# Block rows of the later query thirds: two heads copied by GpSimd, four by VectorE five slots later

## The chip, the cores and the metric

The kernel runs on one core of a Trainium2 chip. A core has five engines, each with an instruction stream of its own that it executes in order: TensorE (PE: matmuls and transposes, with weight loads, PEld, beside them), VectorE (DVE), ScalarE (ACT), GpSimd (POOL) and SyncE (SP, which here only issues DMAs). They wait for each other by semaphores. The metric is the device time of one execution in microseconds (us): 216.38 us, the median of three runs (216.07 to 217.03).

## What is computed

A block-sparse attention followed by a gated MLP with a spatial gate.

```python
# q, k, v: (4, 8, 768, 64) = batch, heads, sequence, head dim
scores = q @ k.T / sqrt(64)
mask   = |blk_i - blk_j| <= 1, or blk_i or blk_j the first or last of 24 blocks of 32,
         or blk_j one of 3 sampled blocks of blk_i      # the same for all batches and heads
attn   = softmax(where(mask, scores, -1e9)) @ v
x      = attn.transpose(0, 2, 1, 3).reshape(4, 768, 512)

h      = relu(x @ w_in)                  # 512 -> 1024
u, v   = h[..., :512], h[..., 512:]
v_n    = (v - mean(v)) / sqrt(var(v) + 1e-6)
v_s    = w_spatial @ v_n + b_spatial     # over the 768 positions
out    = (u * v_s) @ w_out               # float32 (4, 768, 512)
```

## The kernel before

**The mask as 24 more rows.** The scores of a head are matmuls over 88 rows of one tile, `kq` (88 x 8 heads x 1536, bf16): columns 0 to 767 are keys, 768 to 1535 queries. Rows 0 to 63 hold the head's transposed keys and queries. Rows 64 to 87 (`MR`, one for each of the 24 blocks) hold the block rows: for a key the block that it lies in, for a query a large negative number for each block that it may not see. So the product over 88 rows is the masked score, and the exponential follows directly. The block rows are the same for all heads and batches; they are built for head 0 and then copied to the other seven, once, by `rows(hs, cs, eng)` (L239 to L244: heads `hs`, columns `cs`). The rows of `kq` are reused for every later batch, so these copies happen only at the start.

**Thirds.** The 768 queries are cut in three thirds of 256 columns; `qcols(t0, n)` are the query columns of `n` thirds from `t0`. The heads go in pairs: pair 0 is heads 0 and 1, pair 3 heads 6 and 7. For the first batch (four pairs) the scores are made in twelve units of three slots (`UNITS`, L386): units 0 and 1 are the heads 0 and 1 with all thirds; units 2, 3, 4 the first third of pairs 1, 2, 3; units 5, 6, 7 the second third of these pairs; units 8 to 11 the last third of all four. A slot (`qk_unit`, L389) is four matmuls into a PSUM tile of two buffers (`ps`, L405) and one exponential of 1024 columns on ACT into `a_all` (L410). So unit 4 has the slots 12 to 14, unit 5 (heads 2 and 3, second third) the slots 15 to 17, unit 6 (heads 4 and 5) 18 to 20, unit 7 (heads 6 and 7) 21 to 23. From slot 36 on the other batches follow, whole heads at a time (`qk_full`, L418 and L422).

**The order of the work.** It is written out by hand. The loop at L795 issues for each slot `s` the scores; then the products of the exponentials with V that are due (`av_unit`, L451; three groups of eight matmuls for a unit, some slots after its scores), behind the last of which DVE normalizes (a reciprocal, L433, and a multiplication, L434, into `xn`); then what `when(slot, ...)` put down for the slot; then steps of the MLP (`run_queue`; its matmuls are L545); then transposes of finished `xn` (`xtr_third`, L491; PE at L267, copied by DVE at L214 into `xt`, with the result lying in the same PSUM buffer as the products with V). A step that is put down earlier stands earlier in the streams of all the engines that it uses.

What `when` puts down near the change:

- `tr_first(p)` at slots 4, 7, 10 (pairs 1, 2, 3): eight PE transposes (L267) of the pair's keys and first query third into a PSUM bank, and two DVE copies (L214, 64 x 1024 each) into `kq`.
- `tr_rest(p)` at slots 8, 11, 14, 17 (pairs 1, 2, 3, 0): four transposes (two for pair 0) of the later query thirds and two DVE copies (64 x 512 each). These transposes and the MLP's products share two PSUM banks, taken in turn (`moe_tag`); from slot 15 to 20 the first product of the MLP holds one of them.
- `rows` by the list `ROWS` (L693), all on DVE: slots 1, 1, 5, 6 and 9. The entry of slot 9 copies the later two query thirds to heads 2 to 7, 24 x 3072 elements. Within a slot the order is that of the calls: `rows` before `tr_rest`.

**GpSimd's stream** near the change (L305 to L330) is the casts of loaded fp32 data to bf16: `cast` (L134) of keys, queries and V of pairs 1 to 3 into `nat` and `vv`, each behind its DMA, then the rest of pair 0's queries, then the eight casts of `w_in` (L230), of which the loads of the last two wait for the first two casts, and later the next pairs and `w_spatial` (L518). It also made two small `rows` copies earlier (L305, L306). The products with V of unit 3 need pair 2's V cast.

Of the kernel before, what the change touches and what calls it, by code (L numbers as in the profile page):

```python
# [26 lines left out]
def kernel(  # L27
# [58 lines left out]
    K_, Q_ = slice(0, S), slice(S, 2 * S)  # L86

    def qcols(t0, n=1):
        return slice(S + t0 * TW, S + (t0 + n) * TW)
# [4 lines left out]
    def dram(src, p, hs=slice(0, 2), cs=slice(0, NCH)):  # L94
        b, g = divmod(p, NG)
        return src[b, 2 * g + hs.start:2 * g + hs.stop].rearrange(
            "h (p c) d -> p h (c d)", c=NCH)[:, :, cs.start * D:cs.stop * D]
# [5 lines left out]
    def load(p, nm, hs=BOTH, cs=ALLC, eng=nc.sync):  # L103
        if (nm, p) not in st:
            st[nm, p] = work.tile([128, 2, S // 2], FP32, tag="st_" + nm, bufs=3, name="st_" + nm)
        eng.dma_start(out=st[nm, p][:, hs, cs.start * D:cs.stop * D],
                      in_=dram(SRC[nm], p, hs, cs))
# [4 lines left out]
    def nat0_view():  # L112
        return nat[0].rearrange("p c h d -> p (c h d)").rearrange("p (h x) -> p h x", h=2)

    def cast(p, nm, eng, hs=BOTH, cs=ALLC):
        if nm == "v":
            dst = vv[p % NVV][:, hs, cs, 0:D]
        else:
            if p not in nat:
                nat[p] = work.tile([128, 2 * NCH, 2, D], BF16, tag="nat", bufs=4, name="nat")  # L120
            c0 = 0 if nm == "k" else NCH
            dst = nat[p][:, c0 + cs.start:c0 + cs.stop].rearrange("p c h d -> p h c d")[:, hs]
        src = st[nm, p].rearrange("p h (c d) -> p h c d", d=D)[:, hs, cs]
        if p == 0 and nm != "v":
            dst = nat0_view()[:, hs, (c0 + cs.start) * D:(c0 + cs.stop) * D]
            if cs is not C45:
                dst = dst[:, 0].rearrange("p (i t d) -> p t i d", t=2, d=D)
                src = src[:, 0].rearrange("p (t i) d -> p t i d", t=2)
            else:
                dst = dst.rearrange("p h (c d) -> p h c d", d=D)  # L130
        if eng is nc.scalar:
            nc.scalar.activation(out=dst, in_=src, func=AF.Copy)
        else:
            eng.tensor_copy(out=dst, in_=src)  # L134
# [76 lines left out]
    PL, DV = nc.gpsimd, nc.vector  # L211
# [27 lines left out]
    def rows(hs, cs, eng=nc.vector):  # L239
        src = kq[MR, 0:1, cs].to_broadcast([NB, hs.stop - hs.start, cs.stop - cs.start])  # L240
        if eng is nc.scalar:
            nc.scalar.activation(out=kq[MR, hs, cs], in_=src, func=AF.Copy)
        else:
            eng.tensor_copy(out=kq[MR, hs, cs], in_=src)  # L244
# [70 lines left out]
    load(3, "q")  # L315
    cast(3, "k", PL)
    cast(3, "q", PL)
    load(2, "v")
    load(0, "q", cs=C45)
    load(3, "v")  # L320
# [365 lines left out]
    def when(slot, *fns):  # L686
        at.setdefault(slot, []).extend(fns)

    def c(f, *a, **kw):
        return lambda: f(*a, **kw)  # L690

    K_Q0 = slice(0, S + TW)
    ROWS = [(1, 2, 8, qcols(0)), (1, 3, 4, K_), (5, 4, 6, K_), (6, 6, 8, K_), (9, 2, 8, qcols(1, 2))]  # L693
    when(0, second)
    when(1, third)
    when(2, lambda: filler(FILL3, psum.tile([128, 512], FP32, tag=moe_tag(), bufs=1, name="wps")))
    for p, sl in ((1, 4), (2, 7), (3, 10)):
        when(sl, c(tr_first, p))
    for sl, h0, h1, cs in ROWS:
        when(sl, c(rows, slice(h0, h1), cs))  # L700
# [146 lines left out]
```

## Time and profile before

| | us |
|---|---|
| median of three runs | 216.38 |
| the profiled execution | 215.56 |
| its span on the core | 213.8 |
| PE busy in the span | 205.5 (96%) |
| ACT busy | 170.6 (80%) |
| DVE busy | 132.9 (62%) |
| POOL busy | 72.1 (34%) |
| block-row copies on DVE (L244), five of them | 541 to 1433 ns each |
| block-row copies on POOL (L244), two of them | 394 and 821 ns |

The granted clock of PE was 0.999 of full speed. Times in the profile are us from the start of the span, durations in us unless ns is said. A row of the timeline has the start, the length, the engine, the line, the operation, what is written from what with partitions x elements, how many instructions are merged in the row, and in brackets the idle time of the engine before it and what ended it. The chain of waits is followed back from the last instruction, at each step to what released it or to the instruction ahead of it on its engine; "issue" in it is time in which the engine waited for nothing that the profile shows.

### The profile page before, as it was taken

The numbers are of one execution on the slowest core, as the hardware profiler recorded it, in microseconds if no ns is written. First come the engines' busy times: TensorE is split into PE (matmuls) and PEld (weight loads), VectorE is DVE, ScalarE is ACT, GpSimd is POOL, SyncE is SP. The second block draws the span as 40 slices with busy tenths as digits, with TensorE's granted clock in tenths as the row PEclk, the third lists the DMA queues.
The fourth block names the chain that finished last, engine by engine and source line by source line (L and its number), as shares of the span: only waits on it lengthen the run. The fifth ranks groups of instructions, "written<-read, shape, count | busy, mean of one in ns | idle before, by whom it ended". The sixth has DMA issues, their size and how long they took to land.

```text
span 213.8 us, 5290 instructions
## 1 busy us (share of the span) xinstructions
PE 205.5 (96%) x2147; PEld 130.2 (61%) x2147; DVE 132.9 (62%) x286; ACT 170.6 (80%) x226; POOL 72.1 (34%) x118
## 2 busy tenths in 40 slices
PE   8897999999999999999999999999999999999991
PEld 7686878766666666656556655665565565544431
DVE  7899585979554534494986454385874443486540
ACT  6997999999999999979998888979989776275021
POOL 6886669885681412223351040131020000022000
PEclk9999999999999999999999999999999999999999
DMA  5998899999999989899491597894101225500266
GB/s 155 351 373 307 257 339 284 274 229 326 277 362 193 259 268 256 267 308 212 112 224 37 62 316 154 217 317 85 37 3 37 49 52 135 220 29 0 51 148 247
DMA packets 63324, 41.83 MB, mean 196 GB/s; under 512 B 45124, under 2 KB 58052, under 8 KB 63300
## 3 DMA queue, kind: packets, MB, share of 16 engines
q1 hardware_dynamic: 62868, 41.11, 73.9%
q10 hardware_dynamic: 432, 0.39, 0.6%
q8 instruction: 17, 0.28, 0.5%
q14 instruction: 7, 0.06, 0.1%
HBM read 24.38 MB, written 6.29 MB: 143 GB/s over the span
## 4 chain that ended last, share of the span: by engine, by line
PE 89%; DVE 6%; DMA 2%; ACT 1%; issue 0%; DVEq 0%; ACTq 0%
PE ps_moe L545 33%; PE ps L418 22%; PE ps_av L469 13%; PE ps_t L545 6%; PE ps L405 5%; PE ps_av L451 3%; PE ps_sc L545 3%; DVE kq L214 3%; DVE kq L244 2%; DMA gt<-un 2%; PE wps L182 2%; PE ps_av L267 1%; DVE xn L434 1%; ACT osb L217 0%; PE ps L267 0%
## 5 line engine op out<-in xcount | busy, mean ns | idle before, releaser
L422 ACT ACTIVATE a_all<-ps 128x768 bf16<-128x768 f32 x144 | 113.9, 812 | 15.1 <-PE ps L418 7.6
L418 PE MATMUL ps<-kq 88*128 88x384 bf16 x288 | 70.5, 325 | 0.1
L469 PEld LDWEIGHTS <-a_all 128*128 128x128 bf16 x864 | 46.5, 97 | 20.0
L469 PE MATMUL ps_av<-vv,a_all 128*128 128x65 bf16 x864 | 51.2, 194 | 0.0
L418 PEld LDWEIGHTS <-kq 88*128 88x128 bf16 x288 | 28.0, 98 | 31.0 <-issue 0.9
L545 PE MATMUL ps_moe<-w_in_t,xt 128*128 128x512 bf16 x144 | 44.0, 378 | 0.1
L410 ACT ACTIVATE a_all<-ps 128x1024 bf16<-128x1024 f32 x36 | 34.8, 1026 | 2.8 <-PE ps L405 2.6
L545 PE MATMUL ps_moe<-vn,w_spt 128*128 128x512 bf16 x108 | 32.7, 378 | 0.0
L134 POOL CAST nat<-st_k 128x768 bf16<-128x768 f32 (+2 forms) x17 | 13.5, 796 | 42.6 <-DMA st_k<-in_k_dram 42.4
L433 DVE RECIPROCAL rc<-ps_av 128x6 f32<-128x6 f32 (+1 forms) x36 | 6.6, 184 | 29.3 <-PE ps_av L469 27.8
L405 PE MATMUL ps<-kq 88*128 88x256 bf16 (+1 forms) x140 | 21.5, 275 | 2.3 <-DVE kq L214 1.5
L582 POOL TENSOR_SCALAR std<-mv 128x3 f32<-128x3 f32 (+1 forms) x9 | 2.1, 238 | 63.6 <-DVE mv L579 47.5
L613 DVE SCALAR_TENSOR_TENSOR un<-ps_moe,b_col,un 128x512 bf16<-128x512 f32 x18 | 13.5, 749 | 16.2 <-PE ps_moe L545 15.7
L545 PE MATMUL ps_moe<-w_out_t,gt 128*128 128x512 bf16 x72 | 21.5, 378 | 0.0
L545 PEld LDWEIGHTS <-xt 128*128 128x128 bf16 x192 | 15.4, 97 | 7.3 <-issue 0.3
L434 DVE TENSOR_TENSOR xn<-ps_av,rc 128x384 bf16<-128x384 f32 (+1 forms) x36 | 18.5, 513 | 1.2
L578 DVE BATCH_NORM_STATS2 stats<-vn 128x6 f32<-128x512 bf16 x24 | 16.5, 687 | 1.4 <-ACT vn L573 0.9
L405 PEld LDWEIGHTS <-kq 88*128 88x128 bf16 x140 | 12.6, 97 | 6.2 <-DVE kq L214 2.3
L134 POOL CAST nat<-st_q 128x768 bf16<-128x768 f32 (+1 forms) x18 | 14.1, 782 | 5.9 <-DMA st_q<-in_q_dram 5.3
L214 DVE COPY kq<-tt 64x1536 bf16<-64x1536 bf16 x24 | 15.9, 660 | 0.3
L134 POOL CAST vv<-st_v 128x768 bf16<-128x768 f32 x16 | 13.8, 863 | 5.6 <-DMA st_v<-in_v_dram 5.5
L451 PE MATMUL ps_av<-vv,a_all 128*128 128x65 bf16 x288 | 14.8, 194 | 0.0
(81 smaller groups left out, 209.8 us busy)
## 6 DMA issues: line engine op xcount, KB each, us to landing
st_v<-in_v_dram SPq DMA_DIRECT2D x16, 384.0 KB, 5.8
out_dram<-osb SPq DMA_DIRECT2D x23, 256.0 KB, 3.1
st_k<-in_k_dram SPq DMA_DIRECT2D x15, 384.0 KB, 4.5
st_q<-in_q_dram SPq DMA_DIRECT2D x15, 384.0 KB, 5.1
ws_f<-in_moe_w_spatial_dram SPq DMA_DIRECT2D x6, 384.0 KB, 7.2
w_f<-in_moe_w_in_dram SPq DMA_DIRECT2D x8, 256.0 KB, 7.2
w_f<-in_moe_w_out_dram SPq DMA_DIRECT2D x4, 256.0 KB, 4.2
st_q<-in_q_dram SPq DMA_DIRECT2D x2, 128.0 KB, 4.8
```

The source lines that it names most:

```text
L134: eng.tensor_copy(out=dst, in_=src)
L214: nc.vector.tensor_copy(out=o, in_=i)
L405: nc.tensor.matmul(out=ps[:, at:at + n * TW], lhsT=kq[:, h, ci * 128:(ci + 1) * 128], rhs=kq[:, h, qcols(t0, n)], start=True, stop=True)
L410: nc.scalar.activation(out=out, in_=ps, func=AF.Exp, scale=0.125)
L418: nc.tensor.matmul(out=ps[:, hf * 512:hf * 512 + HALF], lhsT=kq[:, j % H, ci * 128:(ci + 1) * 128], rhs=kq[:, j % H, S + hf * HALF:S + (hf ...
L422: nc.scalar.activation(out=a_ref["h", j][:, ci, :].rearrange("p (b c) -> p b c", b=2), in_=ps.rearrange("p (b c) -> p b c", b=2)[:, :, 0:H ...
L434: nc.vector.tensor_tensor(out=out, in0=ps[:, :, 0:D], in1=rc[:, 0:n].to_broadcast([128, n, D]), op=ALU.mult)
L451: nc.tensor.matmul(out=av_ref[u][:, to, :], lhsT=a_ref[u][:, at:at + 128], rhs=vv[pp % NVV][:, h, ci, :], start=(ci == 0), stop=(ci == NCH ...
L469: nc.tensor.matmul(out=av_ref[j][:, qc, :], lhsT=a_ref["h", j][:, ci, qc * 128:(qc + 1) * 128], rhs=vv[p % NVV][:, h, ci, :], start=(ci == ...
L545: nc.tensor.matmul(out=ref["ps"][:, 0:w], lhsT=lhs(i), rhs=rhs(i), start=(i == 0), stop=(i == n - 1))
L578: nc.vector.bn_stats(out=stats, in_=self.vn[:, tcc, :])
L613: nc.vector.scalar_tensor_tensor(out=self.un[:, tcc, :], in0=ps, scalar=b_col[:, tcc:tcc + 1], in1=self.un[:, tcc, :], op0=ALU.add, op1=AL ...
```

## The change

The slot 9 entry of `ROWS` goes. Heads 2 and 3 get their later query thirds by a `rows` call on GpSimd, in its stream behind the casts of pair 3's keys and queries and ahead of the V casts of pairs 2 and 3; heads 4 to 7 get theirs by DVE at slot 14, ahead of pair 3's `tr_rest`.

```diff
@@ -315,6 +315,7 @@
     load(3, "q")
     cast(3, "k", PL)
     cast(3, "q", PL)
+    rows(slice(2, 4), qcols(1, 2), PL)
     load(2, "v")
     load(0, "q", cs=C45)
     load(3, "v")
@@ -690,7 +691,7 @@
         return lambda: f(*a, **kw)
 
     K_Q0 = slice(0, S + TW)
-    ROWS = [(1, 2, 8, qcols(0)), (1, 3, 4, K_), (5, 4, 6, K_), (6, 6, 8, K_), (9, 2, 8, qcols(1, 2))]
+    ROWS = [(1, 2, 8, qcols(0)), (1, 3, 4, K_), (5, 4, 6, K_), (6, 6, 8, K_), (14, 4, 8, qcols(1, 2))]
     when(0, second)
     when(1, third)
     when(2, lambda: filler(FILL3, psum.tile([128, 512], FP32, tag=moe_tag(), bufs=1, name="wps")))
```

What each instruction computes is unchanged; the order of PE's, ACT's and SP's instructions is the same as before. On DVE one copy of 24 x 3072 becomes one of 24 x 2048 that stands further back, and POOL has one copy of 24 x 1024 more.

## The prediction

> **What bounds the kernel now.** I read the page first (TensorE, PE, busy 96% of the span), then the table of stretches, to see where the other 4% lies. Its columns after the stretch are length, busy time of PE, PEld, VectorE (DVE), ScalarE (ACT) and GpSimd (POOL), granted clock, DMA share, GB/s.
>
> ```profile
> 7.00:19.00 12.00, 9.73 (x140) 8.01 (x139) 11.45 (x21) 10.71 (x12) 8.74 (x12) 1.00 1.05 364
> 19.00:44.00 25.00, 24.75 (x362) 20.10 (x360) 18.86 (x50) 23.89 (x25) 19.30 (x32) 1.00 1.01 280
> ```
>
> From 7 to 19 us DVE is busy 11.45 of 12.00 us and PE 9.73: there DVE sets the pace. From 19 to 44 us PE is busy 24.75 of 25.00 us, at full clock. So an engine's time saved before 19 us is worth something if DVE saves it, and it reaches the end only if PE then keeps the lead it got.
>
> Next the chain of waits around the instruction that the change takes out (start, us, what):
>
> ```profile
> 15.92 1.43 DVE kq L244
> 17.35 0.03 issue
> 17.38 0.19 DVE rc L433
> 17.58 0.02 issue
> 17.60 0.42 DVE xn L434
> 18.02 0.60 DVE kq L214
> 18.62 0.05 issue
> 18.67 0.61 PE ps L405 x4
> ```
>
> The 1.43 us at L244 is the copy of 24 x 3072 block rows of slot 9; it lies on the chain. Behind it in DVE's order stand the normalization of head 1 (L433, L434) and the copies of pair 3's transposed keys, for which slot 12's scores (18.67) wait. The timeline of PE and of POOL around it, the idle time before a row in brackets:
>
> ```profile
> 16.43 0.60 PE L405 MATMUL ps<-kq 88*128 88x256 bf16 x4
> 16.87 0.42 PE L451 MATMUL ps_av<-vv,a_all 128*128 128x65 bf16 x8
> 17.13 0.38 PE L267 MATMUL ps<-ident,nat 128*128 128x128 bf16 x4
> 18.67 0.61 PE L405 MATMUL ps<-kq 88*128 88x256 bf16 x4 [1.16 <-DVE kq L214]
> 20.96 0.28 PE L267 MATMUL ps_av<-ident,xn 128*128 128x128 bf16 x2 [0.25 <-DVE xn L434]
> ...
> 14.62 0.83 POOL L134 CAST nat<-st_q 128x768 bf16<-128x768 f32 x1
> 15.71 0.83 POOL L134 CAST vv<-st_v 128x768 bf16<-128x768 f32 x1 [0.27 <-DMA st_v<-in_v_dram]
> 18.48 0.83 POOL L134 CAST vv<-st_v 128x768 bf16<-128x768 f32 x1 [1.93 <-DMA st_v<-in_v_dram]
> 20.71 3.16 POOL L230 CAST w_in_t<-w_f 128x512 bf16<-128x512 f32 x5
> ```
>
> PE loses 1.16 us to that chain, and POOL has a hole of 1.93 us just behind.
>
> **Removed: the slot 9 copy.** Without it the reciprocal waits only for slot 10's AV products, the first eight of the sixteen at 15.47, whose last ends at about 15.89; it starts at 15.93 instead of 17.38. The next L214 copies stand 0.56 us behind the reciprocal (17.94 - 17.38), so DVE would be ready at 16.49, but PE's transposes for pair 3 end at 16.60: the copies start at 16.64 instead of 17.94. DVE gains 17.94 - 16.64 = 1.30 us, not 1.43. Slot 12's scores are then due at 17.37 (the copy's end plus the 0.05 us of issue), and PE has ended slot 11's work by about 17.35 (17.13 plus four at 0.055), so nothing else holds them. After that DVE still leads: its four copies (2.28 us in a row), reciprocal and normalization end 1.30 us earlier, and PE waits for that xn as it did at 20.96. Slot 14 starts at 19.78 instead of 21.08. ACT follows: its exponentials have 1.29 us of idle time before 19.38.
>
> **Added on POOL: heads 2 and 3.** One copy of 24 x 1024. The rows of the same kind are 24x768 in 821 ns and 24x256 in 394 ns, so 0.83 ns an element and 1.03 us (0.82 if it were no dearer than the 768, 1.64 as two of those). It stands behind the cast that ends at 15.45, so it ends at about 16.5 (16.3 to 17.1), and pair 2's V cast (0.83) at 17.3 (17.1 to 17.95) instead of 16.54. The first to need that V is slot 12's second group of AV products, at 19.38 before and 18.07 after the shift: hidden at both ends, price nothing. The V cast of 18.48 waits for its DMA, so everything behind it on POOL keeps its time, and SP's loads that wait for POOL (two w_in loads, behind the casts of 19.59 and 20.15) do too. Slot 15's scores, which read these rows, come after that V in PE's order and need no wait of their own. If the cover went (a copy over 1.75 us), each us more would be lost on PE.
>
> **Added on DVE: heads 4 to 7 at slot 14.** One copy of 24 x 2048, placed between the normalization at 22.19 (20.89 after the shift) and pair 3's later-query copies at 22.53, so it starts at 21.23. Its price depends on POOL: the 3072 copy began during POOL's cast of 15.71 to 16.54 and ended 0.81 us after that cast did; the two 1536 copies at 11.86 took 692 and 541 ns, the first beginning in POOL's cast of 11.31 to 12.14 and ending 0.41 us after it. So a copy waits out the running cast and then costs 0.26 ns an element: 0.54 us for 2048. At 21.23 POOL is in its w_in casts, 0.61 us each: the copy ends between 21.8 (no wait) and 22.42 (one cast waited out), and at 22.66 if it took the whole 1.43 us of the 3072. I take 22.42. The pair 3 copies (0.85 us together) then end at 23.3 where they would have ended at 22.08. Queued behind them are an xt copy (due 22.83, done 23.6), needed by slot 18's AV products at 23.87, and slot 17's transposes of pair 0's last queries, which reuse the PSUM bank of these copies: due at 24.62 - 1.30 = 23.32. Price on PE 0.02 us (0 to 0.3). The w_in casts pushed back by about 0.5 us are needed from 25.9 on (slot 20), and POOL waits for DMA again at 24.86, which gives the time back. Slots 18 and 21, which read heads 4 to 7, come behind that same bank wait.
>
> A rule speaks against the change: the Trainium skill's "Perfetto Trace Analysis", section "Optimizing Scalar/DVE Operations", says that VectorE and GpSimd share a port, so that moving work between the two "might not help". By it the move would save nothing and the sum would be near 0. The trace has this beside it: in the 1 us in which POOL would make that copy DVE has only copies out of PSUM and a normalization, and the L214 copies of 512 took 0.43 us at 15.46, beside a cast, and 0.42 us at 19.80, without one; so the sum keeps its 1.30 us.
>
> **What gives some of it back later.** Casts that wait for DMAs keep their times while PE runs 1.3 us early, so covers shrink. I followed each wait of PE, DVE and ACT from 22 us on. Two matter.
>
> ```profile
> 40.48 0.82 POOL L134 CAST nat<-st_q 128x768 bf16<-128x768 f32 x1
> ...
> 38.19 1.00 DVE L214 COPY kq<-tt 64x1536 bf16<-64x1536 bf16 x1
> 42.14 0.56 DVE L214 COPY kq<-tt 64x1536 bf16<-64x1536 bf16 x1
> 42.62 0.28 DVE L214 COPY xt<-ps_av 128x256 bf16<-128x256 bf16 x1
> 48.26 0.40 DVE L188 TENSOR_SCALAR vn<-vn,mv,rstd 128x512 bf16<-128x512 bf16 x1
> ```
>
> First: the 0.56 us copy of 42.14 moves to 40.84, into POOL's cast of 40.48 to 41.30, and can become like the 1.00 us copy of 38.19, which met casts. The xt copy behind it then ends up to 0.44 us late; slot 36's AV products at 43.09 need it and have 0.19 us of slack (43.09 - 42.90). Price 0 to 0.25 us; I take 0.13. Second: the normalization at 48.26 needs POOL's rstd, done at 48.07 behind weight casts that wait for a DMA (43.38). DVE reaches it at 46.96 and stands until 48.1, so it is 1.15 us late from there; PE next needs its result through the PSUM bank freed at 50.70 and reused at 52.24, 1.54 us of slack. Price nothing, with 0.39 us left. Later covers are wide where POOL or DMA is involved, and PE's tail follows DVE.
>
> **Sum.** 1.30 - 0.02 - 0.13 = 1.15 us. The profiled execution took 215.56 us (span 213.8 and 1.8 around it), which would become 214.4; it is 0.8 below the median of the runs, 216.38 (216.07 to 217.03), which becomes 215.2. A measurement of this kernel can tell about 0.5%, 1.08 us, from no change, so the forecast sits just beyond that bound, at 215.3.
>
> **Rivals.**
> - The lead is eaten by work that DMA times (40 to 52 us). For it: DVE has no idle time from 48.26 to 53.9, and a contended L188 or L214 there costs 0.45 us more (0.90 at 49.05 against 0.40 at 48.26), so two of them beyond the 0.39 us left would cost PE 0.5; with 0.25 at slot 36 the gain is 0.5. Against: those casts keep their places. 215.5 to 216.1.
> - Slower than before: the slot 14 copy doesn't get in between two w_in casts. They run back to back from 19.59 to 23.87; if it must wait for the last, it ends at 24.41, pair 3's copies at 25.27, and slot 17's transposes lose 25.3 - 23.32 = 2.0 us: net 0.7 us slower, 217.1. It decides from a copy that ends at 23.8. For it: the 24x768 copy of 9.41 took 975 ns beside a cast. Against: at 38.19 a copy got in between back-to-back casts after one.
> - The whole 1.30 us or a little more, with no collision at slot 36: 214.6 to 215.1.
>
> **How the numbers follow.** Forecast (215.1 to 215.4) 0.45; whole gain 0.15; eaten lead 0.27; starved copy and what lies above 0.13. The likeliest's time is 215.2. Leaving out some 0.06 below and 0.12 above gives 214.6 to 216.5. Faster by over 0.5%: the whole gain and most of the forecast, less what the spread of the runs takes, 0.53; within: the rest of it, the eaten lead and the smaller part of the starved copy, 0.39; slower: 0.08.
>
> **What would show it.** Right: no L244 copy at 15.9; PE's idle time before slot 12's scores gone and slot 14 at 19.8; a POOL L244 copy of about 1.0 us at 15.5; a DVE L244 copy of 0.6 to 1.2 us at 21.2; slot 17's transposes at 23.3; PE at 48 us 1.1 to 1.3 us early. Wrong: a PE wait for POOL's V cast at slot 12, a wait over 0.3 us at slot 17, new PE waits for DVE at 41.8 or 51 us, or a tail that waits longer for its DMA than before.

## The result, and the profile after

| | before | after |
|---|---|---|
| median, us | 215.95 (16 runs, 215.04 to 218.01) | 214.81 (16 runs, 213.89 to 215.72) |
| ratio, 95% interval | | 0.9937 (0.9917 to 0.9957) |
| the profiled execution, us | 215.56, span 213.8 | 215.18, span 213.4 |
| median, us, compared a second time | 215.79 (27 runs) | 214.94 (10 runs) |
| ratio, compared a second time | | 0.9951 (0.9928 to 0.9974) |

The change makes the kernel faster by 0.5 to 0.6%: 1.36 us by the first ratio (0.9 to 1.8), 1.06 us by the second (0.6 to 1.6). Sixteen runs also put the kernel before at 215.95, 0.43 us below the median of three from which the forecast was carried.

The lines of the changed file from L318 on have moved by one: scores are L406, products with V L452, normalization L434 and L435. The table of stretches of the changed kernel, columns as for before:

```profile
7.00:19.00 12.00, 10.39 (x156) 8.34 (x152) 10.12 (x21) 11.07 (x13) 9.71 (x13) 1.00 1.05 366
19.00:44.00 25.00, 24.75 (x360) 20.00 (x358) 19.63 (x51) 24.27 (x26) 19.70 (x32) 1.00 1.05 291
```

In the first stretch DVE went from 11.45 to 10.12 us busy and PE from 9.73 to 10.39; behind it PE is as full as before (24.75 of 25.00 us). The chain of waits of the changed kernel between slot 9 and slot 12 (start, us, what):

```profile
15.13 0.61 PE ps L406 x4
...
16.94 0.45 PE ps L267 x8
17.39 0.44 PE ps L406 x4
17.83 0.26 PE ps_av L452 x8
18.09 0.22 PE ps L267 x4
18.31 0.47 PE ps L406 x4
```

Here stood the copy at L244, the normalization and the key copies of DVE; now PE follows on itself. The scores of slots 9 and 14 in the kernel before:

```profile
14.34 0.61 PE L405 MATMUL ps<-kq 88*128 88x256 bf16 x4 [0.16 <-DVE kq L214]
...
21.08 0.60 PE L405 MATMUL ps<-kq 88*128 88x256 bf16 x4
```

The timeline of the changed kernel, PE's rows (slots 9, 12 and 14 and the two transposes), then DVE's, then POOL's:

```profile
15.13 0.61 PE L406 MATMUL ps<-kq 88*128 88x256 bf16 x4 [0.47 <-DVE kq L214]
18.17 0.61 PE L406 MATMUL ps<-kq 88*128 88x256 bf16 x4
20.45 0.29 PE L267 MATMUL ps_av<-ident,xn 128*128 128x128 bf16 x2 [0.25 <-DVE xn L435]
20.58 0.60 PE L406 MATMUL ps<-kq 88*128 88x256 bf16 x4
24.12 0.27 PE L280 MATMUL ps<-ident,nat 128*128 128x128 bf16 x2
...
17.43 2.29 DVE L214 COPY kq<-ps 64x1024 bf16<-64x1024 bf16 x4
22.14 0.78 DVE L244 COPY kq<-kq 24x2048 bf16<-24x2048 bf16 x1
22.94 0.85 DVE L214 COPY kq<-ps 64x512 bf16<-64x512 bf16 x2
41.38 0.56 DVE L214 COPY kq<-tt 64x1536 bf16<-64x1536 bf16 x1
...
15.66 0.83 POOL L134 CAST nat<-st_q 128x768 bf16<-128x768 f32 x1 [0.23 <-DMA st_q<-in_q_dram]
16.55 1.03 POOL L244 COPY kq<-kq 24x1024 bf16<-24x1024 bf16 x1
17.65 1.59 POOL L134 CAST vv<-st_v 128x768 bf16<-128x768 f32 x2
39.67 0.82 POOL L134 CAST nat<-st_q 128x768 bf16<-128x768 f32 x1
40.45 0.82 POOL L134 CAST vv<-st_v 128x768 bf16<-128x768 f32 x1
```

Slot 12's scores (18.17) have no idle time before them any more. But all of this stands later on the clock than the prediction has it, because slot 9 began at 15.13 instead of 14.34, before any instruction that the change touches: in this execution the loads of pair 1's queries and pair 0's V landed at 9.32 and 10.37 us, in the one of before at 8.15 and 9.19. So times are compared from the start of slot 9 (first row) on; PE's lead at a slot is by how much less time than before lies between the start of slot 9 and that slot. By that yardstick pair 3's key copies begin 2.30 us after slot 9 (17.43 - 15.13) where it was 3.60, slot 14 begins 5.45 us after it (20.58) where it was 6.74, and PE's lead is 1.30 us at slot 12, 14, 18 and 35 alike and 1.43 at the last exponentials. The last 0.13 us come from one place near 91 us, where DVE copies a later pair's transposed keys and queries beside a POOL cast whose start a DMA sets. These rows are from before, from the changed kernel and from one of the two further profiles of before (e10, last experiment below):

```profile
89.92 0.78 DVE L214 COPY kq<-tt 64x1536 bf16<-64x1536 bf16 x1
89.46 0.83 POOL L134 CAST nat<-st_k 128x768 bf16<-128x768 f32 x1 [7.51 <-DMA st_k<-in_k_dram]
...
89.41 0.64 DVE L214 COPY kq<-tt 64x1536 bf16<-64x1536 bf16 x1
88.82 0.83 POOL L134 CAST nat<-st_k 128x768 bf16<-128x768 f32 x1 [7.42 <-DMA st_k<-in_k_dram]
...
90.64 1.05 DVE L214 COPY kq<-tt 64x1536 bf16<-64x1536 bf16 x1
90.45 0.83 POOL L134 CAST nat<-st_k 128x768 bf16<-128x768 f32 x1 [7.82 <-DMA st_k<-in_k_dram]
92.34 0.59 PE L545 MATMUL ps_moe<-w_in_t,xt 128*128 128x512 bf16 x2 [0.41 <-DVE osb L214]
```

The longer the copy, the later DVE's next copy (`osb`), for which PE waits: 0.14 us in the first profile of before (91.20 to 91.34), 0.41 in e10, nothing in the changed kernel.

### The profile page after: what moved, and what is told of

Its sections match the earlier page's. It is cut to its first block, busy times and chain, and to the rows that moved or that the text cites. A ratio compares the mean times of both kernels' runs of the same rounds, so it can differ in the third digit from the quotient of the medians.

```text
span 213.4 us, 5292 instructions
## 1 busy us (share of the span) xinstructions
PE 205.7 (96%) x2147; PEld 130.1 (61%) x2147; DVE 131.7 (62%) x286; ACT 170.8 (80%) x226; POOL 73.6 (35%) x119
## 4 chain that ended last, share of the span: by engine, by line
PE 91%; DVE 2%; ACT 2%; DMA 2%; issue 0%; ACTq 0%
PE ps_moe L546 33%; PE ps L419 22%; PE ps_av L470 13%; PE ps_t L546 6%; PE ps L406 6%; PE ps_av L452 4%; PE ps_sc L546 3%; DMA gt<-un 2%; PE wps L182 2%; ACT a_all L411 1%; PE ps L267 1%; DVE kq L214 1%; DVE kq L244 1%; PE ps_av L267 1%; ACT osb L217 0%; DVE xn L435 0%
## 5 line engine op out<-in xcount | busy, mean ns | idle before, releaser
L434 DVE RECIPROCAL rc<-ps_av 128x6 f32<-128x6 f32 (+1 forms) x36 | 6.7, 186 | 28.5 <-PE ps_av L470 27.0
L406 PE MATMUL ps<-kq 88*128 88x256 bf16 (+1 forms) x140 | 21.5, 275 | 1.2 <-ACT a_all L411 0.8
L435 DVE TENSOR_TENSOR xn<-ps_av,rc 128x384 bf16<-128x384 f32 (+1 forms) x36 | 18.5, 513 | 1.2
L406 PEld LDWEIGHTS <-kq 88*128 88x128 bf16 x140 | 12.5, 97 | 4.9 <-DVE kq L214 1.0
L452 PE MATMUL ps_av<-vv,a_all 128*128 128x65 bf16 x288 | 14.8, 194 | 0.3 <-POOL vv L134 0.3
```

The lines of the kernel that those rows point to most:

```text
L406: nc.tensor.matmul(out=ps[:, at:at + n * TW], lhsT=kq[:, h, ci * 128:(ci + 1) * 128], rhs=kq[:, h, qcols(t0, n)], start=True, stop=True)
L435: nc.vector.tensor_tensor(out=out, in0=ps[:, :, 0:D], in1=rc[:, 0:n].to_broadcast([128, n, D]), op=ALU.mult)
L452: nc.tensor.matmul(out=av_ref[u][:, to, :], lhsT=a_ref[u][:, at:at + 128], rhs=vv[pp % NVV][:, h, ci, :], start=(ci == 0), stop=(ci == NCH ...
```

## The experiments

All executions with a profile in one table, us; "to the end" is the span less the start of slot 9. The ratios are to the kernel before on the same chip, with their 95% intervals. "Twice more" are two further profiles of the kernel before, the last experiment below. The cuts of the edits are against the changed kernel; "..." stands for what is left out.

| kernel | slot 9 starts | slot 9 to 14 | slot 9 to the end | ratio |
|---|---|---|---|---|
| before | 14.34 | 6.74 | 199.5 | |
| before, twice more | 15.67, 15.54 | 6.26, 6.26 | 199.4, 199.3 | |
| changed, twice | 15.13, 15.15 | 5.45, 5.46 | 198.3, 198.1 | 0.9937 (0.9917 to 0.9957), 0.9951 (0.9928 to 0.9974) |
| e1: POOL part alone | 15.92 | 6.53 | 199.4 | 0.9999 (0.9980 to 1.0017) |
| e2: slot 14 part alone | 14.72 | 6.12 | 198.3 | 0.9960 (0.9937 to 0.9984) |
| e3: all six heads on POOL | 15.49 | 5.45 | 197.6 | 0.9942 (0.9920 to 0.9964) |
| e4: slot 14 copy twice | 14.95 | 5.45 | 198.9 | 0.9975 (0.9957 to 0.9994) |
| e6: xt copy earlier | 15.39 | 4.93 | 198.0 | 0.9951 (0.9926 to 0.9975) |
| e7: pair 3's keys on POOL | 14.32 | 5.75 | 198.6 | 0.9957 (0.9928 to 0.9986) |
| e8 and e11: e6 and e7 together | 14.15, 13.84 | 5.65, 5.25 | 198.6, 197.9 | 0.9922 (0.9896 to 0.9949), 0.9946 (0.9917 to 0.9974) |

### POOL's part alone: e1

Heads 4 to 7 stay at slot 9, on DVE.

```diff
-    ROWS = [..., (14, 4, 8, qcols(1, 2))]
+    ROWS = [..., (9, 4, 8, qcols(1, 2))]
```

> Heads 2 and 3 go to POOL as in the change, but the copy for heads 4 to 7 (24x2048) stays on DVE at slot 9. The yardstick is PE's time from the first score of slot 9 to that of slot 14: 6.74 us in the kernel before, 5.45 us in the changed one. My theory (a DVE copy waits out the POOL instruction that runs, then costs 0.26 ns an element): the POOL copy of 15.5 to 16.5 holds up the DVE copy of 15.92, which ends at about 17.0 instead of 17.35: yardstick 6.4 us, some 0.3 us faster than before. Rival 1 (a copy costs by its elements alone, 1.43 us x 2/3 = 0.95): ends at 16.9, or at 16.5 with 0.56 us at full rate: yardstick 5.9 to 6.3, 0.5 to 0.9 us faster. Rival 2 (the later DMA-timed work eats any lead): no difference in the whole time.

No difference: 0.9999. The timeline of e1, DVE's copy, POOL's work around it, and PE's wait before slot 12:

```profile
17.51 1.22 DVE L244 COPY kq<-kq 24x2048 bf16<-24x2048 bf16 x1
...
16.26 1.03 POOL L244 COPY kq<-kq 24x1024 bf16<-24x1024 bf16 x1
17.36 0.83 POOL L134 CAST vv<-st_v 128x768 bf16<-128x768 f32 x1
...
20.04 0.61 PE L406 MATMUL ps<-kq 88*128 88x256 bf16 x4 [0.93 <-DVE kq L214]
```

A third fewer elements on DVE bought almost nothing. POOL's copy pushed the V cast to 17.36, and DVE's copy, begun at 17.51, ended at 18.73: the cast's end (18.19) and 0.54 us, which is 2048 by the 0.26 ns of the prediction. What POOL took over it handed back as DVE's wait for POOL's cast. Slot 9 to 14 took 6.53 us, 0.21 less than in the first profile of before and 0.27 more than in the two others; a gain of 0.2 us would not show in the ratio, whose interval is 0.4 us wide to each side. So the gain of the changed kernel is not that POOL relieves DVE of some elements: a DVE copy left behind the cast that POOL's copy pushes back gives it away.

### Slot 14's part alone: e2

POOL copies nothing; DVE copies heads 2 and 3 at slot 9, and heads 4 to 7 at slot 14 as in the changed kernel.

```diff
-    rows(slice(2, 4), qcols(1, 2), PL)
...
-    ROWS = [..., (14, 4, 8, qcols(1, 2))]
+    ROWS = [..., (9, 2, 4, qcols(1, 2)), (14, 4, 8, qcols(1, 2))]
```

> No copy on POOL: heads 2 and 3 (24x1024) stay on DVE at slot 9, heads 4 to 7 move to slot 14 as in the change. My theory: POOL's V cast of 15.71 to 16.54 holds the copy up, which then costs 0.27 us: it ends at 16.81 instead of 17.35, yardstick 6.2 us, 0.54 us faster than before, so that the 1024 elements left at slot 9 cost 0.8 us, more than half of what all 3072 cost. Rival (by elements): 1.43 / 3 = 0.48 us, ends at 16.4, yardstick 5.8, 0.95 us faster.

Faster than before by 0.4% (0.86 us, 0.35 to 1.36). Its timeline, DVE, POOL and PE:

```profile
16.30 0.81 DVE L244 COPY kq<-kq 24x1024 bf16<-24x1024 bf16 x1
22.41 0.68 DVE L244 COPY kq<-kq 24x2048 bf16<-24x2048 bf16 x1
...
16.01 0.83 POOL L134 CAST vv<-st_v 128x768 bf16<-128x768 f32 x1 [0.26 <-DMA st_v<-in_v_dram]
...
18.43 0.61 PE L405 MATMUL ps<-kq 88*128 88x256 bf16 x4 [0.53 <-DVE kq L214]
```

The small copy again ended at the cast's end and 0.27 us (16.84, 17.11), and PE still waited 0.53 us before slot 12. Slot 9 to 14 took 6.12 us: between before and changed, as the theory had it. Whether the other half of the gain is worth its 0.67 us (6.12 - 5.45) in the median too, the intervals do not tell; to the end of the span this execution is as short as the changed kernel's (198.3).

### All six heads on POOL: e3

```diff
-    rows(slice(2, 4), qcols(1, 2), PL)
+    rows(slice(2, 8), qcols(1, 2), PL)
...
-    ROWS = [..., (14, 4, 8, qcols(1, 2))]
+    ROWS = [...]
```

> All six heads (24x3072) on POOL, nothing at slot 14. The copy should take 2.6 to 2.75 us (0.83 ns an element), so pair 2's V cast behind it ends at about 19.0 where slot 12's second AV products are due at 18.07. My theory (POOL's copy is free up to about 1.75 us and each us more is lost on PE, less the 0.4 us for which PE waits for xn anyway): PE waits some 1 us for POOL's V cast at slot 12, slot 9 to slot 14 takes about 6.1 us, 0.6 to 0.7 us faster than before and 0.6 to 0.7 slower than the changed kernel. Rival (POOL's stream has slack enough): as fast as the changed kernel, 5.45 us.

The expected loss behind pair 2's V cast did not come: 0.9942, and slot 14 is 5.45 us behind slot 9 as in the changed kernel. Its timeline, POOL and PE:

```profile
15.89 2.74 POOL L244 COPY kq<-kq 24x3072 bf16<-24x3072 bf16 x1
18.70 1.59 POOL L134 CAST vv<-st_v 128x768 bf16<-128x768 f32 x2
...
19.57 0.42 PE L452 MATMUL ps_av<-vv,a_all 128*128 128x65 bf16 x8 [0.18 <-POOL vv L134]
20.81 0.29 PE L267 MATMUL ps_av<-ident,xn 128*128 128x128 bf16 x2
```

The copy (0.89 ns an element) made the V cast late and slot 13 was 0.34 us later than in the changed kernel. But at the last row PE no longer waited for xn, a wait of 0.25 us in the changed kernel. One wait took the place of the other, and nothing was left of it at slot 14. The expectation had priced the first wait without asking what wait stood behind it.

### Slot 14's copy twice: e4

The entry of slot 14 stands in the list twice, so that DVE makes the same copy two times.

```diff
-    ROWS = [..., (14, 4, 8, qcols(1, 2))]
+    ROWS = [..., (14, 4, 8, qcols(1, 2)), (14, 4, 8, qcols(1, 2))]
```

> The changed kernel with the slot 14 copy made twice (the second writes the same rows again). In the changed kernel's profile pair 3's copies end 0.33 us before slot 17's transposes need their bank, and the copy took 0.78 us. My theory: the second copy takes 0.56 us, or 1.1 if it waits out a w_in cast, so slot 17's transposes wait 0.25 to 0.8 us; slot 9 to slot 14 stays 5.45, slot 9 to slot 18 goes from 9.10 (10.39 before) to 9.35 to 9.9, and the whole time is 0.25 to 0.8 us longer than the changed kernel's. Rival (the copy at slot 14 has cover to spare): 9.10 and no difference.

0.9975: against the changed kernel's ratios 0.5 to 0.8 us of the gain are gone, though the intervals touch or overlap; the trace shows the loss itself. The timeline of e4, DVE and PE:

```profile
21.97 2.12 DVE L244 COPY kq<-kq 24x2048 bf16<-24x2048 bf16 x2
24.11 0.85 DVE L214 COPY kq<-ps 64x512 bf16<-64x512 bf16 x2
...
25.02 0.27 PE L280 MATMUL ps<-ident,nat 128*128 128x128 bf16 x2 [0.91 <-DVE kq L214]
```

The wait is where the prediction put the price of a late slot 14 copy: slot 17's transposes, for the PSUM bank of pair 3's copies (24.11 to 24.96). PE's lead over the first profile of before fell there from 1.29 us (slot 17) to 0.23 (slot 18). In the changed kernel those copies end at 23.79 and the transposes begin at 24.12 without waiting: 0.33 us to spare, so the single copy costs nothing. The two copies took 1.11 and 0.98 us, each begun inside one of POOL's w_in casts, which stood back to back from 19.68 to 23.56. The first ended 0.54 us after the cast of 21.93 to 22.54, and POOL's next cast waited for it in turn: a DVE copy gets in after one cast, it is not held up to the last.

### The changed kernel again: e5

> The changed kernel once more, for a second profile of it. The first lost 0.8 us against the kernel before ahead of slot 9, where loads landed up to 1.2 us later. My theory: that is the spread of the loads and not the change; the time from slot 9's first score to slot 14's is 5.45 us again (1.30 less than before), slot 9's start lies anywhere from 14.3 to 15.9 us, and no lead is lost between slot 18 and slot 36. Rival: the change itself delays the start, slot 9 begins at 15 us or later again; or, with earlier loads, the collision that I expected at slot 36 shows as a PE wait of 0.1 to 0.25 us.

0.9951, and from slot 9 to the last exponentials the same within 0.02 us: lead 1.29 us at slot 12, 14, 18 and 35, 1.45 at the last exponentials. In both profiles the copy for slot 36 that I expected to meet a POOL cast took 0.56 us, as before (41.38 in the changed kernel, 41.42 here), and nothing was lost.

### Two further edits: e6, e7 and both

e6 puts the transposes of unit 2's finished rows (`xtr_third(2)`, whose xn PE waits for at 20.45) at slot 14 instead of the end of slot 13, ahead of the block rows.

```diff
+    when(14, c(xtr_third, 2))
...
-        late.setdefault({1: 13, 2: 13}.get(u, 3 * u + 7), []).append(c(xtr_third, u))
+        if u != 2:
+            late.setdefault({1: 13}.get(u, 3 * u + 7), []).append(c(xtr_third, u))
```

> The changed kernel with the transposes of unit 2's xn put down at slot 14, ahead of the row copy, instead of late in slot 13, where PE waits 0.4 us for that xn. My theory (that wait is the last place where DVE holds PE): slot 14 begins 0.4 us earlier against slot 9, 1.6 to 1.7 us less than before instead of 1.30 by slot 16, and the whole time is about 0.35 us shorter than the changed kernel's. Rival (DVE or ACT holds PE a slot later instead): the lead is back to 1.3 us at slot 18, no difference in the whole time.

The wait went and slot 14 came 0.52 to 0.53 us earlier still, but the result of those transposes is needed soon after. PE's row in e6:

```profile
22.11 0.43 PE L452 MATMUL ps_av<-vv,a_all 128*128 128x65 bf16 x8 [0.16 <-DVE xt L214]
```

Slot 15's products stand behind DVE's xt copy; from slot 16 on the lead is 1.38 us against 1.30. The ratio is that of the changed kernel beside it, 0.9951. The wait was moved, not removed.

e7 also gives GpSimd the key block rows of heads 6 and 7 (24x1536), which DVE copied at slot 6, and puts heads 2 and 3 behind pair 2's V cast.

```diff
     cast(3, "q", PL)
-    rows(slice(2, 4), qcols(1, 2), PL)
+    rows(slice(6, 8), K_, PL)
...
     cast(2, "v", PL)
+    rows(slice(2, 4), qcols(1, 2), PL)
...
-    ROWS = [..., (6, 6, 8, K_), (14, 4, 8, qcols(1, 2))]
+    ROWS = [..., (14, 4, 8, qcols(1, 2))]
```

> The changed kernel with one more copy off DVE: the key block rows of heads 6 and 7 (24x1536, slot 6, 0.54 to 1.18 us on DVE in the profiles so far) on POOL behind pair 3's casts, and the POOL copy for heads 2 and 3 behind pair 2's V cast. The all-six copy showed that POOL can hold 2.74 us there at no cost. My theory: DVE comes to slot 12 some 0.5 to 1.1 us earlier; slot 12 then waits for POOL's key rows (due about 16.9) or V cast (17.8), which takes back up to 0.3: 0.3 to 0.8 us faster than the changed kernel. Rival (the start is set by the loads, not by DVE): no difference.

Slot 9 began at 14.32, and slots 12 and 33 paid part of it back. PE's two rows of e7 (its scores are L407, products L453):

```profile
17.90 0.61 PE L407 MATMUL ps<-kq 88*128 88x256 bf16 x4 [0.32 <-POOL kq L244]
39.76 0.41 PE L453 MATMUL ps_av<-vv,a_all 128*128 128x65 bf16 x8 [0.25 <-DVE xt L214]
```

Its ratio, 0.9957 (0.9928 to 0.9986), is not told apart from the changed kernel's. Both edits in one kernel:

> The two last edits together. If they are independent: 0.35 + 0.3 to 0.8, so 0.6 to 1.1 us faster than the changed kernel, some 0.9% faster than the kernel before. If PE's wait for xn at slot 13 is what paid for the late V cast, as with all six heads on POOL, the V cast's delay shows on PE at slot 12 and the sum is only about 0.4 us.

> The two further edits together, once more: 0.8% faster than the kernel before the first time (6 runs), against 0.5 to 0.6% for the changed kernel. If that is real it is 0.7 to 0.9% again, slot 9 begins near 14.2 us as it did (the copy that met POOL's casts is gone from slot 6), and slot 9 to slot 18 is 0.65 us shorter than before. If it was the spread of the loads: 0.5 to 0.6%.

0.9922 and then 0.9946, medians 214.41 and 214.54 us: lower than the changed kernel's each time, but with intervals that overlap. A version that beats it beyond doubt was not found. From slot 9 to slot 18 they took 9.75 and 9.35 us, more than the changed kernel's 9.10; what they have over it is an early slot 9, at 14.15 and 13.84.

### The kernel before, twice more: e9 and e10

No edit. The yardstick had so far compared several executions with one execution of the kernel before.

> The kernel before once more, for its profile. In its first profile slot 9 began at 14.34 us, in the two profiles of the changed kernel at 15.13 and 15.15. Theory: where slot 9 begins is set by when the loads land and by how the DVE copies of slots 5 and 6 meet POOL's casts, so it varies from execution to execution (14.3 to 15.9); slot 9 to slot 14 is 6.74 us within 0.1. Rival: the kernel before begins slot 9 at 14.3 always and the change delays it by 0.8 us.

> The same again: theory, slot 9 begins between 14.3 and 15.9 us and not at the same time as in the other two profiles; slot 9 to slot 14 6.7 us. Rival: 14.3 a third time.

They took 216.87 and 216.55 us, above the median of 215.8 beside them as the first was below it. The start of slot 9 does vary (15.67, 15.54), but the 6.7 us behind it that I expected did not come: they differ from the first profile in the very place. The timeline of e9, DVE, POOL and PE:

```profile
17.26 0.95 DVE L244 COPY kq<-kq 24x3072 bf16<-24x3072 bf16 x1
...
16.25 0.83 POOL L134 CAST vv<-st_v 128x768 bf16<-128x768 f32 x1 [0.26 <-DMA st_v<-in_v_dram]
...
19.52 0.61 PE L405 MATMUL ps<-kq 88*128 88x256 bf16 x4 [0.68 <-DVE kq L214]
```

And of e10:

```profile
17.12 0.95 DVE L244 COPY kq<-kq 24x3072 bf16<-24x3072 bf16 x1
...
17.57 1.20 POOL L134 CAST vv<-st_v 128x768 bf16<-128x768 f32 x1 [1.78 <-DMA st_v<-in_v_dram]
...
19.39 0.61 PE L405 MATMUL ps<-kq 88*128 88x256 bf16 x4 [0.68 <-DVE kq L214]
```

In the first profile the copy began 0.62 us before the end of the V cast and took 1.43 us. In e9 it began 0.18 us behind that cast, in e10 ahead of it, and took 0.95 both times; PE waited 0.68 us instead of 1.16, and slot 9 to 14 took 6.26 us instead of 6.74. So what the change removes is worth 1.30 us on PE at slot 14 in an execution of the first kind and 0.81 (6.26 - 5.45) in one of the other. How often each kind comes is not shown.

## Why the prediction was right or wrong

**The mechanism was right.** The copy of slot 9 was what PE waited for before slot 12. It went, the wait went with it, and the next thing to hold PE was its own work, as the sum had it. DVE's later copy and POOL's copy cost PE nothing, and the lead was kept to the last exponentials.

**Removed, 1.30 us: right for the execution it was read from, too large for others.** Both profiles of the changed kernel lead that execution by 1.30 and 1.29 us. But 0.48 us of it was a wait for POOL's cast that the two other executions of before didn't have; against them the lead at slot 14 is 0.81 us. It grows to 1.22 at the last exponentials, since e10 lost 0.41 us at the collision near 91 us, and e9 0.25 there and the rest before 55 us. The prediction did not see this one: it looked for collisions that the lead brings, not for one that is gone when PE and DVE come earlier. That the load of that cast came at another time too is a rival that no run here separates. Over the whole stretch from slot 9 to the end of the span the three executions of before average 199.4 us and the two of the changed kernel 198.2, 1.2 us apart, which is also the middle of the two measured gains. That the sum of 1.15 us agrees so well is in part luck.

**The lock between DVE and POOL: right.** End of the running cast and 0.26 ns an element holds for 1024, 2048 and 3072 elements (e2, e1, before), and for the copy at slot 14 too: the cast before it ended at 22.38, the copy at 22.92. Without a cast the copy is dearer than the prediction's 0.26 ns alone: 0.54 us for 1536, 0.68 for 2048, 0.95 for 3072, which is 0.14 us and 0.26 ns an element. The Trainium skill's "SBUF — State Buffer", section "Who interferes with whom", has the same rule for VectorE instructions in a two-port mode: whoever issues first gets the port pair that VectorE shares with GpSimd for the whole instruction, and the other blocks. The ports themselves no run here shows. In e10 it goes the other way: the V cast begun at 17.57 inside the copy ended at 18.77, 0.70 us after the copy.

**POOL's copy, 1.03 us and no price: right,** to the hundredth. The cover was wider than told: a copy of 2.74 us (e3), beyond the 1.75 us from which it was to cost, was paid for by the xn wait that followed.

**DVE's copy at slot 14, price 0.02 (0 to 0.3): the price held, the length was too long.** It took 0.78 and 0.68 us, because it began near the end of a cast; the 1.2 us taken are the case in which it begins with one (1.11 in e4). It left 0.33 us before slot 17's transposes. The place was right: e4 pays there.

**The collision at slot 36, 0.13: wrong.** The step said that casts which wait for DMAs keep their times. They didn't: the query cast of 40.48 came at 39.67 and at 39.66, counted from slot 9 1.6 us earlier, more than PE's own lead. The V cast behind it (40.45 to 41.27) was over when DVE's copy began at 41.38, by 0.11 us. The change need not be the reason: in the three executions of before the query cast came 26.1, 23.2 and 24.9 us after the start of slot 9, so its place could not be carried over from one profile. As a whole, the case that came true on PE is the rival with the whole gain and no collision.

**The wait for rstd at 48 us, priced nothing: right.** PE's lead was no smaller behind it.

**The time, 215.2 against 214.81: the step that failed is the start, not the gain.** The measured time lies below the forecast's 215.1 to 215.4, in the band of the rival with the whole gain (214.6 to 215.1). The gain of 1.15 us lies inside both measured intervals, and the medians of the first comparison lie 1.14 us apart. But the prediction took it from 216.38 us, the median of three runs, and so put the profiled execution 0.8 us below the median; sixteen runs gave 215.95, and these 0.43 us are the whole of the difference. The two wrong terms of the sum, 0.13 at slot 36 that did not come and a removed copy that is not always 1.43 us long, pulled in opposite directions.

**A reading that was wrong.** Where the prediction weighs the rule that speaks against the change, it sets a DVE copy of 0.43 us beside a cast and one of 0.42 at 19.80 "without one". POOL's w_in casts ran there too (from 19.59 on). The conclusion stands by other rows of the same profile: a 64x1024 copy out of PSUM took 0.67 us with a cast beside a fifth of it (17.94) and 0.68 to 0.69 inside casts (10.42, 18.64), and the multiplication into `xn` 0.42 us with and without one.

**The rivals.** The eaten lead is out: PE kept 1.30 us past 60 us. So is the starved copy: DVE got in between POOL's casts each time, even with two copies in a row. The Trainium skill's "Perfetto Trace Analysis", section "Optimizing Scalar/DVE Operations", warns that a move between VectorE and GpSimd might not help. e1 is such a case, 0.9999 (no gain that shows), because a DVE copy was left where POOL's moved work collided with it; the changed kernel and e3 are not: none was left.

## What to carry to other kernels

When work is moved from VectorE to GpSimd, look at what VectorE does while GpSimd makes it: copies within SBUF meet the lock and can give the gain back (24x2048: 1.22 us in e1, 0.68 without a cast), copies out of PSUM and the attention's normalizations did not (0.67 to 0.69 and 0.42 us either way). A copy's length in one profile may hold a wait for a neighbour that the next execution hasn't got; profile the kernel before more than once before a term of half a microsecond is put into a sum. And time a change from the first instruction that it can touch: here slot 9 itself moved by 1.6 us from execution to execution with the same instructions ahead of it, more than the change is worth, while the lead behind it repeated to 0.02 us in the two executions of the changed kernel.

## What the runs showed that I had not expected

- The start spreads most. In ten executions with the same instructions up to slot 9 (before, changed, e1 to e6) slot 9 began at 14.34 to 15.92 us. The loads differ already: pair 1's queries landed at 8.15 to 9.32 us in them. The execution from which the prediction was made had the earliest slot 9 of all ten. It was also the only one in which slot 6's copy of 24x1536 began just ahead of a POOL cast (12.47, 12.52) and took 0.54 us; begun inside one it took 1.17 in the nine others. In the three executions in which POOL made that copy (e7, e8, e11) slot 9 began at 13.84 to 14.32. Behind the last exponentials the executions spread again: 33.8 to 34.4 us to the end of the span.
- What a small DVE copy costs beside GpSimd depends more on how much of the running cast is left than on its size: 24x1024 took 0.81 us in e2, 24x2048 0.68 us there and 1.22 in e1, 24x3072 0.95 or 1.43.
- A longer wait can cost nothing if it stands ahead of another one (e3), and a wait that is taken away can come back a slot later (e6). Both are read from the row behind the wait, not from the wait.
